# Retention and a bilinear feed-forward in one kernel: 64-token chunks in quarters of the array, smaller tiles, stores on another queue

## The chip, the cores and the metric

The kernel runs on one core of a Trainium2 chip. A core has a matrix engine (TensorE, PE in the profile; its weight loads are shown as PEld), three engines for elementwise work (VectorE or DVE, ScalarE or ACT, GpSimd or POOL), a sync engine (SP) that here only issues DMAs, and 16 DMA engines behind the queues. Every engine works through its own instructions in order; semaphores tie them together. The metric is the device time of one execution in microseconds; shorter is better.

## The reference

The first half is a linear attention with decay (retention): 4 batches, 8 heads, 768 tokens, head size 64. The second half is a feed-forward without a nonlinearity other than a product.

```python
gamma = 1.0 - 2.0 ** (-5.0 - np.arange(H))
for t in range(S):
    state = gamma * state + einsum('bhd,bhe->bhde', k[:, :, t], v[:, :, t])
    y[:, :, t] = scale * einsum('bhd,bhde->bhe', q[:, :, t], state)
x = y.transpose(0, 2, 1, 3).reshape(B * S, H * D)   # 3072 x 512
out = ((x @ w_a) * (x @ w_b)) @ w_out               # d_ff = 1536
```

Inputs and output are float32; the kernel multiplies in bfloat16.

## The kernel before, in words

**Slots.** The 3072 tokens are cut into 24 slots of 128 tokens (six for each batch). The decay is put into the operands: k is multiplied by a table of gamma to the power of minus the position, q by the inverse table and the scale, so that the recurrence becomes a plain sum. For a slot, three products are wanted. `scores` (L252) multiplies transposed k and q of the slot, and DVE applies the causal mask while it copies the result out of PSUM (L257, tile aT). `update` (L268) adds the slot's k-v product to the running state of the batch, and a copy (`cast`, L179 on ACT, L181 on DVE) makes a bfloat16 version of it, gst. `inter` (L288) multiplies q by the state from the slots before, `intra` (L297) the masked scores by v; both add into the PSUM tile y. `leave` (L306) copies y on ACT into xt, the transposed input of the feed-forward. Slots 0 to 5 are handled in pairs by other functions (`scores2`, `update2` and so on), which the change leaves alone.

**Where the operands come from.** SP loads k, q and v of a slot (L91), POOL scales k and q (L209, tile kqb) and copies v (L181): `casts`. The transposed form kqT is made in one of two ways. For slots below `ON_PE` = 10, `flip` transposes on TensorE (L234, L236) and DVE copies the result (L238). For the others `casts` issues a DMA transpose on SP (L223), and behind it the loads of slot t + 2. The first loads, up to slot 11, are issued early and in the order of `LOADS`. There are buffers for the raw loads of three pairs of slots, and for six slots of kqb, v and kqT.

**Feed-forward.** `TILES` = 4, 2, 4, 4, 4, 4, 2 groups the slots into tiles of 512 or 256 tokens. For each tile J and each of twelve blocks ft of the 1536 inner columns, `ffn_ab` makes a (four matmuls L446, copied to asb by ACT, L449) and g (four matmuls L456), and DVE multiplies them into ht (L458). Then `ffn_out` makes 128 tokens of the output for each slot i of the tile (twelve matmuls L481), ACT copies them to osb (L179), and a store follows. All of a, g, o, the flips' results and part of the scores share the PSUM pool psff with three buffers of one bank, in turn.

**Order.** Each engine's order is the order of the calls: `seq` ties every instruction to the one before it on its engine. Attention for slots 6 to 23 runs in blocks, `turn(new, old)`: update and scores for the two slots from `new`, inter and intra for the two from `old`, which had their scores in the block before. A hand-written list says before which call of `ffn_ab` or `ffn_out` each block and each flip stands; `run` puts the casts up to four calls ahead of the flip.

**Stores.** For J < 2 they are held and issued by SP at the next call (`store`, L469); after that they are issued at once on ACT's queue (L491), so they stand among ACT's copies. osb has four buffers.

Of the kernel before, what the change touches and what calls it, by code (L numbers as in the profile page):

```python
# [24 lines left out]
def kernel(  # L25
# [38 lines left out]
    osbp = ctx.enter_context(tc.tile_pool(name="osbp", bufs=4))  # L64
# [98 lines left out]
    mask = const.tile([P, 1, P], BF16, name="mask")  # L163
    gst = [const.tile([P, HP, D], BF16, name=f"gst{i}") for i in range(4)]

    def late_tables():
        seq(nc.gpsimd.memset(mask, 1.0))
        seq(nc.gpsimd.affine_select(out=mask, in_=mask, compare_op=ALU.is_ge, fill=0.0, base=0,
                                    pattern=[[0, 1], [1, P]], channel_multiplier=-1))
        tables([[P, NCH], [0, 1]], 1)  # L170
# [45 lines left out]
    def casts(t):  # L216
# [4 lines left out]
        if t >= ON_PE:  # L221
            kqT[t] = tra.tile([P, 2, HP, P], BF16, tag="kqT", name="kqT", bufs=6)
            seq(nc.sync.dma_start_transpose(  # L223
                out=kqT[t].rearrange("p a b c -> p (a b) c"),
                in_=kqb[t].rearrange("p a hp r d -> p (a hp r d)")))
            if t + 2 < NSLOT:
                load_slot(t + 2)

    def flip(t):
        if t >= ON_PE:  # L230
            return
# [11 lines left out]
    def scores(t, ff):  # L243
        if ff:
            at = [psff.tile([P, HP, P], F32, tag="ff", name=f"at{r}") for r in range(2)]
        else:
            both = psat.tile([P, 2, HP, P], F32, tag="at", name="at")
            at = [both[:, r] for r in range(2)]
        for hp in range(HP):
            for c in range(2):  # L250
                for r in range(2):
                    seq(nc.tensor.matmul(at[r][half(c), hp, :], kqT[t][half(r), 0, hp, half(c)],  # L252
                                         kqT[t][half(r), 1, hp, :], start=True, stop=True,
                                         skip_group_check=True))
        aT[t] = tra.tile([P, 2, HP, P], BF16, tag="aT", name="aT")
        for r in range(2):
            seq(nc.vector.tensor_tensor(aT[t][:, r], at[r], mask.to_broadcast([P, HP, P]), op=ALU.mult))  # L257

    def update(t, eng):
        ci = t % NCH  # L260
        if ci == NCH - 1:
            return
        if ci == 0:
            state[0] = psst.tile([P, HP, D], F32, tag="st", name="st")
        st = state[0]
        for hp in range(HP):
            for r in range(2):
                seq(nc.tensor.matmul(st[half(r), hp, :], kb[t][:, hp, r, :],  # L268
                                     vb[t][:, HP * r + hp, :],
                                     start=(ci == 0 and hp == 0), stop=(hp == HP - 1),  # L270
                                     skip_group_check=True))
        cast(eng, gst[(t + 1) % 4], st)
# [3 lines left out]
    def begin(t, *q):  # L276
        fresh = (t // 2, *q) not in begun
        begun.add((t // 2, *q))
        return fresh

    def inter(t):
        if t % NCH == 0:
            return
        for j in range(2):
            for c in range(2):
                for r in range(2):
                    hp = 2 * j + c
                    seq(nc.tensor.matmul(ys[t // 2][r][half(c), 2 * (t % 2) + j, :],  # L288
                                         gst[t % 4][half(r), hp, :], kqT[t][half(r), 1, hp, :],
                                         start=begin(t, c, r), stop=False, skip_group_check=True))  # L290

    def intra(t):
        for r in range(2):
            for j in range(2):
                for c in range(2):
                    hp = 2 * j + c
                    seq(nc.tensor.matmul(ys[t // 2][r][half(c), 2 * (t % 2) + j, :],  # L297
                                         vb[t][:, HP * r + hp, :], aT[t][:, r, hp, :],
                                         start=begin(t, c, r), stop=True, skip_group_check=True))

    def leave(t):
        J, i = where[t]
        if i == 0:
            xt[J] = xtp.tile([P, KT, 4 * P], BF16, tag="xt", name="xt")
        for r in range(2):
            seq(nc.scalar.copy(  # L306
                xt[J][:, 2 * r : 2 * r + 2, i * P : (i + 2) * P].rearrange(
                    "p j (s n) -> p j s n", s=2),
                ys[t // 2][r].rearrange("p (s j) n -> p j s n", s=2)))

    def turn(new, old, eng=nc.scalar):
        if old is not None:
            ys[old // 2] = [psat.tile([P, 4, P], F32, tag=f"y{r}", name="y") for r in range(2)]
        if new is not None:
            update(new, eng)
            scores(new + 1, True)
            scores(new, False)
        if old is not None:
            inter(old)
            inter(old + 1)  # L320
        if new is not None:
            update(new + 1, nc.scalar)
# [307 lines left out]
```

## Time and profile before

| | |
|---|---|
| median of 3 runs | 233.76 us (233.73 to 234.46) |
| the profiled execution | 235.14 us, of which the span of the instructions is 233.4 us |
| mean granted TensorE clock | 1.000 |
| PE, DVE, ACT, POOL busy | 97%, 41%, 36%, 33% of the span |
| moved by DMA | 38.59 MB in 91894 packets |

The page gives the busy time of each engine and a strip of 40 slices, in which each digit is the busy share in tenths. Groups of instructions have the kernel's line, engine, operation, tiles written and read, shapes, count, busy time, the mean of one, and the idle time of the engine before them with what ended it. A timeline has the start, the busy time, the engine and line, and the count of merged instructions. On lines of a queue (SPq, ACTq) the time is that which issuing the DMA took.

### The profile page before, as it was taken

Reading aid. Unit: us, or ns where it says so; the run is one execution under the profiler, and the core shown is the slowest. Engines: PE = TensorE matmul, PEld = TensorE weight load, DVE = VectorE, ACT = ScalarE, POOL = GpSimd, SP = SyncE. Lnnn points to the kernel's source line nnn. Section 1 sums busy time; section 2 is a strip of 40 time slices with the busy share of each in tenths; the row PEclk is TensorE's granted clock in tenths of the full one; section 3 lists DMA queues with packets and bytes.
Section 4 is the critical chain, followed back from the end, with each engine's and each line's share of the span. In section 5 each row is a group of like instructions: output and inputs, shape, how many; then the busy total and the mean of one; then the engine's idle time right before and its main releaser. Section 6 shows DMA issues by size and latency. Waiting matters only on the chain.

```text
span 233.4 us, 5089 instructions
## 1 busy us (share of the span) xinstructions
PE 226.6 (97%) x2094; PEld 125.8 (54%) x2094; DVE 95.7 (41%) x170; ACT 84.5 (36%) x166; POOL 77.4 (33%) x100
## 2 busy tenths in 40 slices
PE   7999999999999999999799999999999999999995
PEld 6667445686554444545354544454544444445874
DVE  3785267543642274614164630164720233310530
ACT  3454436342134433414244523353422343322422
POOL 4347666788664336444454530000000000000000
PEclk9999999999999999999999999999999999999999
DMA  6999999999999999999999972200002200012102
GB/s 173 290 332 352 341 278 361 363 212 222 204 195 263 277 217 228 177 220 220 249 243 203 234 113 90 93 1 3 0 3 90 90 0 3 0 45 90 48 0 90
DMA packets 91894, 38.59 MB, mean 165 GB/s; under 512 B 71776, under 2 KB 87392, under 8 KB 91872
## 3 DMA queue, kind: packets, MB, share of 16 engines
q1 hardware_dynamic: 89280, 33.69, 64.8%
q10 hardware_dynamic: 2592, 4.59, 5.9%
q8 instruction: 16, 0.26, 0.5%
q14 instruction: 6, 0.05, 0.1%
HBM read 28.31 MB, written 6.29 MB: 148 GB/s over the span
## 4 chain that ended last, share of the span: by engine, by line
PE 74%; DMA 10%; SPq 7%; POOL 3%; ACT 1%; issue 1%; DVE 1%; ACTq 0%; POOLq 0%
PE g L456 22%; PE a L446 21%; PE o L481 19%; DMA kf<-in_k_dram 8%; SPq L223 4%; PE idle L432 4%; SPq L91 3%; POOL kqb L209 3%; DMA qf<-in_q_dram 2%; PE at L252 1%; PE y L297 1%; PE y L412 1%; PE tp L348 1%; PE st L268 1%; PE at L364 1%
## 5 line engine op out<-in xcount | busy, mean ns | idle before, releaser
L458 DVE TENSOR_TENSOR ht<-g,asb 128x512 bf16<-128x512 f32 (+1 forms) x86 | 52.0, 605 | 108.9 <-PE g L456 83.7
L456 PE MATMUL g<-xt,wb_bf 128*128 128x512 bf16 (+1 forms) x344 | 75.4, 344 | 1.6 <-ACT asb L449 1.4
L446 PE MATMUL a<-xt,wa_bf 128*128 128x512 bf16 (+1 forms) x344 | 75.9, 345 | 0.4 <-DVE xt L181 0.3
L449 ACT CAST asb<-a 128x512 bf16<-128x512 f32 (+1 forms) x86 | 44.2, 517 | 72.2 <-PE a L446 69.1
L481 PE MATMUL o<-wo_bf,ht 128*128 128x512 bf16 (+2 forms) x312 | 64.2, 363 | 0.0
L456 PEld LDWEIGHTS <-wb_bf 128*128 128x128 bf16 x344 | 33.6, 98 | 30.2 <-issue 2.1
L446 PEld LDWEIGHTS <-wa_bf 128*128 128x128 bf16 x344 | 32.7, 98 | 28.1 <-DVE xt L181 0.6
L481 PEld LDWEIGHTS <-ht 128*128 128x128 bf16 x312 | 29.2, 98 | 31.5
L209 POOL TENSOR_TENSOR kqb<-kf,ktab 128x512 bf16<-128x512 f32 x22 | 22.9, 1043 | 33.9 <-DMA kf<-in_k_dram 33.4
L179 ACT COPY osb<-o 128x512 f32<-128x512 f32 (+2 forms) x25 | 14.1, 565 | 53.5 <-PE o L481 41.5
L257 DVE TENSOR_TENSOR aT<-at,mask 128x512 bf16<-128x512 f32 x36 | 22.3, 682 | 0.0
L209 POOL TENSOR_TENSOR kqb<-qf,qtab 128x512 bf16<-128x512 f32 x18 | 18.8, 1043 | 3.9 <-DMA qf<-in_q_dram 3.1
L181 POOL CAST vb<-vf 128x512 bf16<-128x512 f32 x24 | 14.5, 612 | 11.6 <-DMA vf<-in_v_dram 9.8
L432 PE MATMUL idle<-zero 128*128 128x256 f32 x30 | 10.4, 487 | 1.6 <-DVE zero L125 1.3
L306 ACT CAST xt<-y 128x512 bf16<-128x512 f32 x18 | 9.7, 589 | 3.0 <-PE y L297 3.0
L432 PEld LDWEIGHTS idle<-zero 128*128 128x128 f32 x30 | 6.7, 243 | 2.9 <-DVE zero L125 1.2
L370 DVE TENSOR_TENSOR aT<-at,mask 128x512 bf16<-128x512 f32 x12 | 7.4, 683 | 1.2 <-PE at L364 1.2
L181 POOL CAST wa_bf<-wsta 128x1024 bf16<-128x1024 f32 (+1 forms) x7 | 6.4, 920 | 3.5 <-DMA wsta<-in_moe_w_a_dram 3.5
L181 POOL CAST wb_bf<-wstb 128x1024 bf16<-128x1024 f32 (+1 forms) x7 | 6.4, 920 | 3.4 <-DMA wstb<-in_moe_w_b_dram 3.4
L181 POOL CAST wo_bf<-wsto 128x1024 bf16<-128x1024 f32 x6 | 6.3, 1042 | 2.4 <-DMA wsto<-in_moe_w_out_dram 2.4
L179 ACT CAST gst<-st 128x256 bf16<-128x256 f32 x12 | 4.5, 372 | 6.7 <-PE st L268 6.7
L252 PE MATMUL at<-kqT 64*64 64x128 bf16 x288 | 5.8, 219 | 0.0
(51 smaller groups left out, 86.8 us busy)
## 6 DMA issues: line engine op xcount, KB each, us to landing
kf<-in_k_dram SPq DMA_DIRECT2D x18, 256.0 KB, 4.3
qf<-in_q_dram SPq DMA_DIRECT2D x18, 256.0 KB, 4.9
vf<-in_v_dram SPq DMA_DIRECT2D x18, 256.0 KB, 5.0
out_dram<-osb ACTq DMA_DIRECT2D x17, 256.0 KB, 2.0
wsta<-in_moe_w_a_dram SPq DMA_DIRECT2D x6, 512.0 KB, 8.7
wstb<-in_moe_w_b_dram SPq DMA_DIRECT2D x6, 512.0 KB, 8.7
wsto<-in_moe_w_out_dram SPq DMA_DIRECT2D x6, 512.0 KB, 9.4
kf<-in_k_dram SPq DMA_DIRECT2D x3, 512.0 KB, 7.1
```

The lines of the kernel that those rows point to most:

```text
L179: seq(nc.scalar.copy(dst, src))
L181: seq(engine.tensor_copy(dst, src))
L209: seq(eng.tensor_tensor(dst, src, tab, op=ALU.mult))
L223: seq(nc.sync.dma_start_transpose(out=kqT[t].rearrange("p a b c -> p (a b) c"), in_=kqb[t].rearrange("p a hp r d -> p (a hp r d)")))
L257: seq(nc.vector.tensor_tensor(aT[t][:, r], at[r], mask.to_broadcast([P, HP, P]), op=ALU.mult))
L306: seq(nc.scalar.copy(xt[J][:, 2 * r : 2 * r + 2, i * P : (i + 2) * P].rearrange("p j (s n) -> p j s n", s=2), ys[t // 2][r].rearrange("p ( ...
L432: seq(nc.tensor.matmul(idle[:, : 2 * P], zero[:, :P], zero, start=True, stop=True, skip_group_check=True))
L446: seq(nc.tensor.matmul(a, wa_bf[:, kt, fs], xcols(J, kt, c0, c1), start=(kt == 0), stop=(kt == KT - 1)))
L449: seq(nc.scalar.copy(asb, a))
L456: seq(nc.tensor.matmul(g, wb_bf[:, kt, fs], xcols(J, kt, c0, c1), start=(kt == 0), stop=(kt == KT - 1)))
L458: seq(nc.vector.tensor_tensor(ht[J][:, ft, c0:c1], g, asbs.pop((J, ft, c0)), op=ALU.mult))
L481: seq(nc.tensor.matmul(o, ht[J][:, ft, i * P : (i + 1) * P], wo_bf[:, ft, c0:c1], start=(ft == 0), stop=(ft == NFT - 1)))
```

## The change

It has five parts.

- From slot 6 on, the attention works on 64-token chunks. `chunk_states` replaces `update`: it makes the k-v product of each of the four chunks in two PSUM tiles (one from the pool psst, one from psff), and DVE adds each product to the running sum, kept in float32 in SBUF. The copy to gst (now eight buffers) is put on a list, `later`. `scores` makes only the 64 x 64 diagonal parts; the mask is 64 columns wide. `inter` and `intra` give each half of the slot its own PSUM bank, y0 or y1. All these matmuls use 64 rows by 64 columns of the array and 64 moving columns.
- `inter` is called twice. In the first call (`swap`) the upper rows of the array write the bank of the second chunk and the other way round; in the second call each writes its own. Between them stands `fenced`: a copy of one column on ACT (on DVE in one block) that waits for the last matmul of the first call, and for which the first matmuls of the second call wait. `chunk_states` and `scores` of the new pair stand in between.
- `later` is worked off by `catch_up`: two entries after each `ffn_ab`, all at `ffn_out` and at the next block. `leave` is put there too.
- Tiles are 4, 2, 2, 2, 2, 4, 4, 4 slots, and a new table `ahead` says what stands before which call: (J, ft) is `ffn_ab`, (J, "o", i) is `ffn_out`. Stores of all but the last two tiles are held and issued by SP at the next call; those of the last two tiles are issued by SP at once, except one part of the very last. osb lives in the buffers of the weight loads, eight in all.
- `ON_PE` is 8: slots 8 and 9 get DMA transposes. The first loads end with slot 10, and behind the transpose of slot t come the loads of slot t + 3.

```diff
-TILES = [4, 2, 4, 4, 4, 4, 2]
+TILES = [4, 2, 2, 2, 2, 4, 4, 4]
-ON_PE = 10
+ON_PE = 8
-LOADS = "p0 p1 w0 w1 w2 w3 w4 p2 w5 o0 o1 o2 o3 o4 o5 s6 s7 s8 s9 s10 s11".split()
+LOADS = "p0 p1 w0 w1 w2 w3 w4 p2 w5 o0 o1 o2 o3 o4 o5 s6 s7 s8 s9 s10".split()
...
-            if t + 2 < NSLOT:
-                load_slot(t + 2)
+            if t + 3 < NSLOT:
+                load_slot(t + 3)
...
+    def catch_up(n=100):
+        for fn in later[:n]:
+            fn()
+        del later[:n]
...
+    def chunk_states(n):
+        u = [psst.tile([P, 2, HP, D], F32, tag="st", name="st"),
+             psff.tile([P, 2, HP, D], F32, tag="ff", name="st")]
+        for s in range(2):
+            for hp in range(HP):
+                for c in range(2):
+                    if (n + s + 1) % NCH == 0 and c == 1:
+                        continue
+                    for r in range(2):
+                        seq(nc.tensor.matmul(u[c][half(r), s, hp, :], kb[n + s][half(c), hp, r, :],
+                                             vb[n + s][half(c), HP * r + hp, :],
+                                             start=True, stop=True, skip_group_check=True))
+        for s in range(2):
+            t = n + s
+            sums[t] = tra.tile([P, 2, HP, D], F32, tag="qk"[s] + "T2", name="sums", bufs=2)
+            for c in range(2):
+                if (t + 1) % NCH == 0 and c == 1:
+                    continue
+                new = sums[t][:, c]
+                old = sums[t][:, 0] if c else sums.get(t - 1, sums[t])[:, 1]
...
+                    seq(nc.vector.tensor_tensor(new, u[c][:, s], old, op=ALU.add))
+                later.append(lambda i=2 * t + c + 1, new=new: cast(nc.scalar, gst[i % 8], new))
...
+    def scores(n):
+        at = psat.tile([P, 2, 2, HP, D], F32, tag="at", name="at")
...
+                        seq(nc.tensor.matmul(at[half(c), r, s, hp, :],
+                                             kqT[n + s][half(r), 0, hp, half(c)],
+                                             kqT[n + s][half(r), 1, hp, half(c)],
+                                             start=True, stop=True, skip_group_check=True))
...
+    def fenced(eng):
+        bi = seq(eng.copy(mark, bq) if eng is nc.scalar else eng.tensor_copy(mark, bq))
+        tc.add_manual_dep(bi.ins, last[mybir.EngineType.PE].name, after, reason="rows change banks")
+        return bi.ins
...
+    def inter(o, swap):
+        for s in range(2):
+            for j in range(2):
+                for r in range(2):
+                    c = 1 - r if swap else r
+                    t = o + s
+                    if t % NCH == 0 and c == 0:
+                        continue
+                    for hp in (2 * j, 2 * j + 1):
+                        into(o, c, r, seq(nc.tensor.matmul(
+                            ys[o][c][half(hp % 2), s, 2 * r + j, :], gst[(2 * t + c) % 8][half(r), hp, :],
+                            kqT[t][half(r), 1, hp, half(c)], start=begin(o, c, hp % 2), stop=False,
+                            skip_group_check=True)))
...
     def turn(new, old, eng=nc.scalar):
+        catch_up()
         if old is not None:
+            ys[old] = [psat.tile([P, 2, KT, D], F32, tag=f"y{c}", name="y") for c in range(2)]
+            inter(old, True)
+            fence[old, 0] = fence[old, 1] = fenced(eng)
         if new is not None:
+            chunk_states(new)
+            scores(new)
+        if old is not None:
+            inter(old, False)
+            intra(old)
             for c in range(2):
+                later.append(lambda c=c: leave(old, c))
...
-        osb = osbp.tile([P, DM], F32, tag="osb", name="osb")
+        osb = wstage.tile([P, DM], F32, tag="w" + "ab"[i % 2], name="osb")
...
-            if J < 2:
+            if J < len(TILES) - 2:
                 held.append((dst, src))
             else:
-                seq((nc.sync if c0 else nc.scalar).dma_start(out=dst, in_=src))
+                seq((nc.scalar if ends and not c0 else nc.sync).dma_start(out=dst, in_=src))
...
+    ahead = {
+        (1, 6): [(casts, 6)], (1, 9): [(flip, 6), (casts, 7)], (0, "o", 0): [(flip, 7)],
+        (0, "o", 1): [(turn, 6, None)], (0, "o", 2): [(casts, 8)], (0, "o", 3): [(casts, 9)],
+        (1, "o", 1): [(turn, 8, 6, D_), (casts, 10)],
+        (2, 2): [(casts, 11)], (2, 7): [(casts, 12)], (2, "o", 0): [(turn, 10, 8), (casts, 13)],
+        (3, 0): [(casts, 14)], (3, 6): [(casts, 15)], (3, "o", 0): [(turn, 12, 10), (casts, 16)],
+        (4, 0): [(casts, 17)], (4, 6): [(turn, 14, 12), (casts, 18)],
+        (4, "o", 0): [(turn, 16, 14), (casts, 19)], (4, "o", 1): [(casts, 20)],
+        (5, 2): [(casts, 21)], (5, 5): [(turn, 18, 16), (casts, 22)], (5, 8): [(casts, 23)],
+        (5, "o", 0): [(turn, 20, 18)], (6, 6): [(turn, 22, 20)], (6, "o", 0): [(turn, None, 22)],
+    }
```

More of the change, by code (lines that the diff above doesn't have):

```diff
@@ L274 @@
-    ys, begun = {}, set()
[L276 to L284, printed above, removed]
-            for c in range(2):
[L286 to L290, printed above, removed]
@@ L311, in turn @@
[L311 to L322, printed above, removed]
[L323 to L326 removed]
+    later = []
```

151 lines of the change are left out of this document (69 added, 82 removed).

## The prediction

> **What bounds the kernel now.** I read the page first (parts 1 and 2), then the groups of instructions by form, then the timeline of TensorE around the attention work, and last the timelines of SP and ACT.
>
> ```profile
> span 233.4 us, 5089 instructions
> PE 226.6 (97%) x2094; PEld 125.8 (54%) x2094; DVE 95.7 (41%) x170; ACT 84.5 (36%) x166; POOL 77.4 (33%) x100
> ...
> PEclk9999999999999999999999999999999999999999
> DMA  6999999999999999999999972200002200012102
> ```
>
> TensorE is busy in 97% of the span at the full granted clock, and no other engine in half of it. The DMA engines are nearly full for the first 23 of 40 slices, about 134 us. So two things can set the time: how long TensorE needs for its work, and whether data reach it in time in the first 134 us.
>
> ```profile
> L481 PE MATMUL o<-wo_bf,ht 128*128 128x512 bf16 x276 | 61.6, 379 | 0.0
> L458 DVE TENSOR_TENSOR ht<-g,asb 128x256 bf16<-128x256 f32 x28 | 11.9, 425 | 22.6 <-PE g L456 11.5 <-ACT asb L449 11.1
> L257 DVE TENSOR_TENSOR aT<-at,mask 128x512 bf16<-128x512 f32 x36 | 22.3, 682 | 0.0
> L179 ACT COPY osb<-o 128x128 f32<-128x128 f32 x1 | 0.3, 266 | 1.0 <-PE o L481 1.0
> ```
>
> A mean duration of a matmul holds its way through the array, so what counts is the distance between starts. The timeline of TensorE in one full attention block (slots 18, 19 with 16, 17) shows it; columns are start, busy us, instruction and count:
>
> ```profile
> 130.07 0.38 PE L456 MATMUL g<-xt,wb_bf 128*128 128x512 bf16 x1
> 130.38 0.32 PE L268 MATMUL st<-vb,kqb 128*64 128x64 bf16 x8
> 130.63 0.64 PE L252 MATMUL at<-kqT 64*64 64x128 bf16 x32
> 131.10 0.39 PE L288 MATMUL y<-kqT,gst 64*64 64x128 bf16 x16
> 131.42 0.32 PE L268 MATMUL st<-vb,kqb 128*64 128x64 bf16 x8
> 131.57 0.62 PE L297 MATMUL y<-aT,vb 128*64 128x128 bf16 x16
> 132.12 0.39 PE L446 MATMUL a<-xt,wa_bf 128*128 128x512 bf16 x1
> ```
>
> The block takes 132.12 - 130.38 = 1.74 us, and the last g matmul before it holds 0.31 where one of 512 columns needs 0.216: 0.09 more on entering the block. The busy time per window of all eleven blocks after slot 5 (the first, the last, and the sum of widths):
>
> ```profile
> 60.88:61.96 1.08, 1.08 (x49) 0.89 (x49) 0.73 (x2) 0.59 (x1) 1.08 (x2) 1.00 1.13 257
> 189.19:190.11 0.92, 0.92 (x34) 0.74 (x33) 0.69 (x1) 0.00 (x1) 0.00 (x0) 1.00 0.00 0
> sum 15.40, PE 15.37 PEld 13.12 DVE 12.05 ACT 6.29 POOL 6.19; mean PE 1.40 PEld 1.19 DVE 1.10 ACT 0.57 POOL 0.56
> ```
>
> With entries that is 15.40 + 11 x 0.09 = 16.4 us of TensorE, and PE fills it.
>
> **The change part by part. A, the quarters.** Every attention matmul becomes 64 rows by 64 columns of the array with 64 moving columns, four at a time. Count for slots 6 to 23: chunk_states 264, scores 288, inter 264 (both calls), intra 288: 1104, or 276 rounds of four. What does a round cost? No row has four quarters with 64 columns. Upper end: L252 has four quarters with 128 columns, 32 in (131.10 - 130.63) = 0.47 us, eight rounds of about 57 ns with 0.02 of entry. Lower end: 64 x 64 with 64 columns, two quarters at a time:
>
> ```profile
> 38.52 0.42 PE L383 MATMUL st<-vb,kqb 64*64 64x64 bf16 x16
> ...
> L383 PE MATMUL st<-vb,kqb 64*64 64x64 bf16 x80 | 2.2, 193 | 0.0
> ```
>
> The sixteen starts spread over 0.42 - 0.19 = 0.23 us, seven steps of 33 ns for two. Quarters of L252 run beside each other without lengthening a round, so I take 33 ns for four, the row with the same shape: 276 x 0.033 = 9.1 us. With ten blocks entered at 0.09 + 0.02 it is 10.2. A gains 16.4 - 10.2 = 6.2 us; at 57 ns it would be 16.8, a loss of 0.4.
>
> [...]
>
> **B, flips.** Slots 8 and 9 lose eight transposes each on PE and a copy on DVE:
>
> ```profile
> 65.01 0.39 PE L234 MATMUL tp<-ident,kqb 128*128 128x128 bf16 x4
> 65.23 0.39 PE L236 MATMUL tp<-ident,kqb 128*128 128x128 bf16 x4
> 65.45 0.38 PE L481 MATMUL o<-wo_bf,ht 128*128 128x512 bf16 x1
> ```
>
> 65.45 - 65.01 = 0.44 us each, a gain of 0.9. DVE's copy is off the path.
>
> **C, stores leave ACT.** Rows of PE and ACT at two tile ends:
>
> ```profile
> 113.36 1.03 PE L446 MATMUL a<-xt,wa_bf 128*128 128x512 bf16 x4
> 115.63 0.81 PE L456 MATMUL g<-xt,wb_bf 128*128 128x512 bf16 x3 [1.24 <-ACT asb L449]
> ...
> 111.83 0.59 ACT L179 COPY osb<-o 128x512 f32<-128x512 f32 x1 [2.00 <-PE o L481]
> 114.61 0.34 ACTq L491 DMA_DIRECT2D out_dram<-osb  x1
> 114.99 1.07 ACT L449 CAST asb<-a 128x512 bf16<-128x512 f32 x2 [2.57 <-DMA qf<-in_q_dram]
> ...
> 214.73 0.60 PE L456 MATMUL g<-xt,wb_bf 128*128 128x256 bf16 x4
> 215.17 0.60 PE L446 MATMUL a<-xt,wa_bf 128*128 128x256 bf16 x4
> 215.97 0.60 PE L456 MATMUL g<-xt,wb_bf 128*128 128x256 bf16 x4 [0.20 <-ACT asb L449]
> ```
>
> The store issued on ACT waited for the completion of a q load, and the asb copy stood behind it. From a (113.36) to g (115.63) are 2.27 us instead of 4 x 0.216 = 0.86: 1.4 lost. At 215.17 it is 0.80 instead of 0.44: 0.4 lost. On SP, one block later, nothing of ACT stands behind a store: 1.8 gained. It could be 0 if the same copies were late for another reason.
>
> **D, tiles.** One 512-column tile becomes two of 256. Four matmuls take 215.17 - 214.73 = 0.44 against half of 0.864, 0.005 more, for 48 groups of four: 0.2 lost.
>
> **E, the bank fence.** Between the two inter calls ACT (DVE once) must see the last matmul of the first call, copy one column, and release PE. The smallest copy shown is 266 ns for 128 columns; one column cannot be longer. With 0.19 for the matmul to end and about 0.05 at each handover that is 0.45 to 0.55 us. Meanwhile PE starts chunk_states and scores, 14 to 16 rounds, 0.46 to 0.53. So eight fences are hidden (at worst 0.1 each), and the ninth, in the last block with nothing between, costs 0.45. If ACT is late with something else, all of inter and intra wait: nothing in the before trace is on ACT at those moments but asb, which ends before g does.
>
> **F, DVE and the three ff buffers.** chunk_states takes one ff buffer and hands it back after four adds (256 columns, 0.425 by the L458 row), then two aT (0.682), then the next ht. For tiles of 512 PE is busy elsewhere for longer; for the block inside a 256 tile, before (4, 6), it is not. Adds start 0.9 after the block's start (entry 0.11, inter and chunk_states eight rounds each, 0.24 until DVE sees them), end at 2.6, aT at 4.0, ht at 4.4. PE is at the second a at 1.15 + 0.87 = 2.0 and waits 0.6, and at the third a 0.87 after that, waiting 0.9. Some 0.2 for the gst and leave copies on ACT: 1.7, and 0.1 each before (5, 5) and (6, 6): 1.9 lost, between 0 (adds shorter than ht) and 2.5.
>
> **G, where slot 9 comes from.** Rows of PE, POOL and SP, and the landing row of the DMA transposes:
>
> ```profile
> 55.16 2.75 PE L481 MATMUL o<-wo_bf,ht 128*128 128x512 bf16 x12
> ...
> 60.81 1.04 POOL L209 TENSOR_TENSOR kqb<-qf,qtab 128x512 bf16<-128x512 f32 x1
> ...
> 61.41 0.94 SPq L91 DMA_DIRECT2D kf<-in_k_dram  x1
> 63.57 1.14 SPq L91 DMA_DIRECT2D vf<-in_v_dram  x1
> 64.81 1.09 SPq L469 DMA_DIRECT2D out_dram<-osb  x1
> 66.00 1.50 SPq L223 DMA_TRANSPOSE kqT<-kqb  x1
> ...
> DMA to landing us min/median/max: 3.1/4.7/7.9
> ```
>
> Up to the loads of slot 10, SP's order is unchanged and SP is free at 61.4 (61.41 is the first load of slot 11). Behind it stand now: store of (0, o, 0), 1.1; transpose of slot 8, 1.55; loads of slot 11, 64.81 - 61.41 = 3.4; store of (0, o, 1), 1.1; only then the transpose of slot 9, at 61.4 + 7.15 = 68.6, landing 4.7 later at 73.3. POOL had slot 9 ready at 61.9, and ACT the two outputs by 59.0 and 62.2, so the queue alone decides. PE arrives thus: 55.16, flip 7 0.44, five out blocks of 2.59, the first new block with 16 rounds 0.65, makes 69.2; entry, 12 inter matmuls, chunk_states and slot 8's scores add 0.6: 69.8. In the order of instructions scores(9) then holds all of PE: 73.3 - 69.8 = 3.5 us lost. Bounds: none if the issues take 0.5 to 0.6 and the landing 3.1; 6.7 at a landing of 7.9. I take the median. The next pair (10, 11) is due at 87; the same count puts its second transpose at about 81 and 85.5 landed, so it is met by 2 us, later ones by more, since each pair is due about 15 us after its predecessor where SP needs about 5 us a slot.
>
> Sum: A -6.2, B -0.9, C -1.8, D +0.2, E +0.45, F +1.9, G +3.5 = -2.85. The profiled execution took 235.14 us (span 233.4), 1.4 above the median 233.76 of the runs; the terms are differences, so 232.3 against the former and 230.9 against the latter. I forecast 231.0.
>
> **Rivals.** First, on the other side: a round of four keeps a cost set by feeding pairs of weight load and matmul, not by columns. It turns slower where a round exceeds 33 + 2850 / 276 = 43 ns; at L252's 57 the time is 231.0 + 6.6 = 237.6. For it: L252 at eight instructions in 57 ns is the densest long stretch shown, and 33 asks for nearly twice that; a block has 256 instructions. Against it: L252's starts sit 4 apart inside a round, so the array takes them faster than that.
>
> Second, slot 9 is in time: G is 0 to 1, the time 227.5 to 228.5. For it: landings of 3.1 occur; against it: DMA is full there and SP's issues stretched from 0.6 to over 1 us.
>
> Third, the wait of G cools TensorE: the longest gap shown is 1.24 us at a clock of 9 tenths or more, so no row tests 3.5. If the next out block ran at half clock, its 2.59 us would double: 231.0 + 2.6 = 233.6, no change. [...]
>
> Fourth, several fences or F's buffers wait longer than worked out, 2 to 3 us together: 233 to 234.
>
> **How the numbers follow.** Forecast 0.42; slot 9 in time 0.14; slow rounds 0.24 (over 43 ns three quarters of it); clock 0.08; fences and buffers 0.12. About 0.3% (0.7 us) is what a measurement can tell from no change. Faster holds the first, the second and some of the rest: 0.60; same 0.09; slower 0.31. The likeliest case's own range is 229.5 to 232.5. From 228.0 to 236.0 leaves out part of the second case and the slowest rounds.
>
> **What would show it.** A: starts of the score matmuls in a block about 0.26 us apart for 32, and a block of some 1.2 us. C: no wait for ACT at 113 and 215. E: no wait for ACT in blocks but the last. F: waits of about 1.5 us for DVE after the block before (4, 6). G: one wait of 2 to 5 us for the transpose DMA near 70 us. The forecast is wrong if rounds take over 40 ns, if a second transpose is late, or if fences wait in every block.

## The result and the profile after

Over four runs each, the changed kernel takes 231.48 us (230.93 to 231.91) and the kernel before 234.11 us (233.73 to 234.63): a ratio of 0.9883, 95% interval 0.9857 to 0.991. The forecast was 231.0 from 228.0 to 236.0, faster. The sum behind it, though, holds two large errors that nearly cancel: the quarters gained some 2 us less than worked out, and the late transpose of slot 9, which was to cost 3.5 us, cost nothing.

The profiled execution took 231.07 us, 0.4 below its median, where that of before had 235.14, 1.0 above the median of its four runs. So the pair of profiles is 4.1 us apart and the medians 2.6. The page of the changed kernel, parts 1 and 2:

```profile
span 229.2 us, 6225 instructions
PE 222.2 (97%) x2606; PEld 132.4 (58%) x2606; DVE 97.9 (43%) x193; ACT 95.0 (41%) x207; POOL 78.0 (34%) x101
...
PEclk9999999999999999999999999999999999999999
DMA  6999999999599998999999938002200002100022
```

TensorE is still the bound, at the full clock, with 512 more matmuls and 4.4 us less busy time. The DMA strip has dips (5, 8) within its first 20 slices that the strip of before does not have.

**The blocks.** The timeline of TensorE around the block before (5, 5), which answers the one shown of before at 130 us (start, busy us, instruction, count). `chunk_states` is L261 here, `scores` L284, `inter` L325, `intra` L336:

```profile
135.23 1.03 PE L492 MATMUL g<-xt,wb_bf 128*128 128x512 bf16 x4
136.19 0.32 PE L325 MATMUL y<-kqT,gst 64*64 64x64 bf16 x16
136.34 0.43 PE L261 MATMUL st<-vb,kqb 64*64 64x64 bf16 x32
136.59 0.49 PE L284 MATMUL at<-kqT 64*64 64x64 bf16 x32
136.91 0.34 PE L325 MATMUL y<-kqT,gst 64*64 64x64 bf16 x16
137.06 0.51 PE L336 MATMUL y<-aT,vb 64*64 64x64 bf16 x32
137.50 1.04 PE L482 MATMUL a<-xt,wa_bf 128*128 128x512 bf16 x4
```

The entry costs 136.19 - 135.23 - 4 x 0.216 = 0.10, as before. The block then takes 1.31 instead of 1.74. `chunk_states` needs 0.25 for eight rounds of four, 31 ns a round; `scores` needs 0.32, 40 ns a round; `intra` 0.44 with the way out of the block. The starts of single matmuls show why: for about 48 matmuls they come in bursts of four, 3 to 4 ns apart, a burst every 32 ns; after that one by one, 8.3 ns apart, with a step of 17 to 34 ns every so often. Four steps of 8.3 are 33 ns too, so it is the longer steps, here called pauses, that cost. Busy time per window over all ten blocks (first, one full, last, sum of widths):

```profile
58.38:59.08 0.70, 0.70 (x66) 0.66 (x65) 0.18 (x1) 0.55 (x1) 0.47 (x2) 1.00 0.15 34
136.19:137.50 1.31, 1.31 (x130) 1.27 (x129) 1.03 (x3) 0.19 (x1) 0.00 (x0) 1.00 0.00 0
183.43:184.55 1.12, 0.82 (x65) 0.67 (x64) 0.69 (x1) 0.19 (x1) 0.00 (x0) 1.00 0.00 0
sum 11.89, PE 11.59 PEld 11.06 DVE 8.33 ACT 3.54 POOL 1.33; mean PE 1.16 PEld 1.11 DVE 0.83 ACT 0.35 POOL 0.13
```

With ten entries of 0.09 the attention costs 12.8 us of TensorE where it cost 16.4: 3.6 gained, the last fence included.

**The last fence.** The same view at the last block:

```profile
183.43 0.32 PE L325 MATMUL y<-kqT,gst 64*64 64x64 bf16 x16
184.05 0.32 PE L325 MATMUL y<-kqT,gst 64*64 64x64 bf16 x16 [0.30 <-ACT lgr L302]
184.19 0.43 PE L336 MATMUL y<-aT,vb 64*64 64x64 bf16 x32
184.55 1.25 PE L519 MATMUL o<-wo_bf,ht 128*128 128x512 bf16 x5
```

From 183.43 to 184.05 pass 0.62 where sixteen matmuls need 0.15, so 0.45 to 0.5 is lost, as worked out. No other block has a wait for the fence (L302; lgr is the tile that its copy writes). Behind this wait the next 48 matmuls go in clean rounds of 32 ns.

**Slot 9.** SP's issues and TensorE's rows around the first block with scores of slots 8 and 9 (on SP's lines the time is what issuing took):

```profile
59.15 0.36 SPq L506 DMA_DIRECT2D out_dram<-osb  x1
59.60 1.35 SPq L224 DMA_TRANSPOSE kqT<-kqb  x1
...
63.35 0.77 SPq L506 DMA_DIRECT2D out_dram<-osb  x1
64.22 1.44 SPq L224 DMA_TRANSPOSE kqT<-kqb  x1
...
69.99 0.45 PE L284 MATMUL at<-kqT 64*64 64x64 bf16 x32
```

The order is the one worked out, but it stands 4.4 us earlier: the transpose of slot 9 is issued at 64.22, not 68.6, and landed at 69.25, 0.85 us before its scores. SP even waits for ACT's first output from 56.2 to 59.15. The loads in front of it ran faster: the last load of slot 10 landed at 59.47, against 65.06 in the profile of before.

**The ff buffers.** TensorE behind the block before (4, 6):

```profile
114.65 0.60 PE L492 MATMUL g<-xt,wb_bf 128*128 128x256 bf16 x4
115.75 0.61 PE L482 MATMUL a<-xt,wa_bf 128*128 128x256 bf16 x4 [0.50 <-DVE sums L275]
116.19 0.60 PE L492 MATMUL g<-xt,wb_bf 128*128 128x256 bf16 x4
117.27 0.60 PE L482 MATMUL a<-xt,wa_bf 128*128 128x256 bf16 x4 [0.47 <-DVE ht L494]
```

Four matmuls of 256 columns take 0.43 to 0.44, so 115.75 - 114.65 loses 0.66 and 117.27 - 116.19 loses 0.64; a third loss of 0.19 follows at 119.3. Together 1.5 of the 1.9 forecast. The two other blocks named there have no such wait. A new one of 0.11 stands ahead of (2, 0).

At no tile's end does TensorE wait for ACT any more.

### The profile page after: what moved, and what is told of

It reads as the page before. It is cut to its first block, busy times and chain, and to the rows that moved or that the text cites. A ratio compares the mean times of both kernels' runs of the same rounds, so it can differ in the third digit from the quotient of the medians.

```text
span 229.2 us, 6225 instructions
## 1 busy us (share of the span) xinstructions
PE 222.2 (97%) x2606; PEld 132.4 (58%) x2606; DVE 97.9 (43%) x193; ACT 95.0 (41%) x207; POOL 78.0 (34%) x101
## 4 chain that ended last, share of the span: by engine, by line
PE 93%; DVE 4%; issue 1%; ACT 0%
PE o L519 27%; PE g L492 27%; PE a L482 27%; PE idle L468 3%; PE y L325 2%; PE y L336 1%; PE at L284 1%; DVE aT L406 1%; PE st L261 1%; DVE qT L182 1%; PE at L400 1%; DVE kqb L210 1%; PE y L448 1%; PE tp L384 1%; DVE aT L290 1%
## 5 line engine op out<-in xcount | busy, mean ns | idle before, releaser
L494 DVE TENSOR_TENSOR ht<-g,asb 128x256 bf16<-128x256 f32 (+1 forms) x98 | 53.7, 549 | 98.6 <-PE g L492 83.1
L482 PE MATMUL a<-xt,wa_bf 128*128 128x256 bf16 (+1 forms) x392 | 78.0, 323 | 1.3 <-DVE sums L275 0.5
L492 PE MATMUL g<-xt,wb_bf 128*128 128x256 bf16 (+1 forms) x392 | 77.5, 323 | 0.1
L485 ACT CAST asb<-a 128x256 bf16<-128x256 f32 (+1 forms) x98 | 46.4, 473 | 72.6 <-PE a L482 71.9
L482 PEld LDWEIGHTS <-wa_bf 128*128 128x128 bf16 x392 | 37.6, 98 | 26.2 <-issue 1.0
L492 PEld LDWEIGHTS <-wb_bf 128*128 128x128 bf16 x392 | 38.3, 98 | 24.1 <-issue 0.4
L182 POOL CAST vb<-vf 128x512 bf16<-128x512 f32 x24 | 15.4, 649 | 35.2 <-PE y L336 11.2
L180 ACT CAST gst<-sums 128x256 bf16<-128x256 f32 x33 | 12.9, 406 | 4.0 <-DVE sums L275 2.0
L275 DVE TENSOR_TENSOR sums<-st,sums 128x256 f32<-128x256 f32 x30 | 12.7, 423 | 1.4
L468 PE MATMUL idle<-zero 128*128 128x256 f32 x30 | 10.6, 493 | 1.3 <-DVE zero L124 1.3
L290 DVE TENSOR_TENSOR aT<-at,mask 128x512 bf16<-128x512 f32 x18 | 11.5, 679 | 0.0
L406 DVE TENSOR_TENSOR aT<-at,mask 128x512 bf16<-128x512 f32 x12 | 7.4, 681 | 1.0 <-PE at L400 1.0
```

The lines of the kernel that those rows point to most:

```text
L180: seq(nc.scalar.copy(dst, src))
L182: seq(engine.tensor_copy(dst, src))
L275: seq(nc.vector.tensor_tensor(new, u[c][:, s], old, op=ALU.add))
L290: seq(nc.vector.tensor_tensor(aT[n][:, r].rearrange("p s h d -> p (s h) d"), at[:, r].rearrange("p s h d -> p (s h) d"), mask.to_broadcast ...
L468: seq(nc.tensor.matmul(idle[:, : 2 * P], zero[:, :P], zero, start=True, stop=True, skip_group_check=True))
L482: seq(nc.tensor.matmul(a, wa_bf[:, kt, fs], xcols(J, kt, c0, c1), start=(kt == 0), stop=(kt == KT - 1)))
```

## The experiments

Two theories stand against each other on the result. Theory one, from the profile above: the quarters lost 2 us of their gain to a pace that only the first 48 or so matmuls of a block keep, slot 9 is in time, and the waits at (4, 6) are the only large new ones. Its rivals: slot 9 only just hits, by chance of this run; the pace is set by operands and not by supply; the gain of the stores is as large in the median as in one profile.

**The change again, unaltered.**

> The changed kernel once more, unaltered, with a profile beside runs of the kernel before on the same chip. In its first profile the loads landed 4 to 5 us earlier near 55 us than in the profile of before, and slot 9's transpose landed at 69.25, 0.9 us ahead of its use. If the speed of the loads differs from execution to execution, this profile shows the transpose's landing move with the landing of slot 10's last load (59.5 there), and wherever it lands after 70.1, a wait of TensorE at the scores of slot 9 of just that difference; the time then grows by the same. If the early landing belongs to the kernel, the landing is again near 69.3 and the time 0.988 of before.

231.6 us (230.94 to 232.19), ratio 0.9883 (0.9844 to 0.9921). The transpose of slot 9 landed at 69.91 and was used near 70.7: in time by about the same margin. The waits behind (4, 6) were 0.47, 0.64 and 0.19. So the profile of after is no exception.

**Slots 8 and 9 transposed on TensorE again.**

```diff
-ON_PE = 8
+ON_PE = 10
...
-            if t + 3 < NSLOT:
-                load_slot(t + 3)
+        if t >= 8 and t + 3 < NSLOT:
+            load_slot(t + 3)
...
-        (1, "o", 1): [(turn, 8, 6, D_), (casts, 10)],
+        (1, "o", 0): [(flip, 8), (flip, 9)], (1, "o", 1): [(turn, 8, 6, D_), (casts, 10)],
```

> Slots 8 and 9 are transposed on TensorE again, both right before the last output block ahead of their attention block; the loads of slots 11 and 12 stay where they are. Theory one (transpose in time): TensorE does 0.9 us more, the time is 0.9 us above the changed kernel. Theory two (the queue makes the transpose late, as predicted): the wait of up to 3.5 us goes, the time is up to 2.6 us below the changed kernel, and the profile of the unaltered kernel shows that wait.

232.41 us (231.52 to 232.69), 0.9906 (0.987 to 0.9942): 0.8 above the unaltered change on the same chip, though the intervals overlap. In the profile the two flips take from 67.33 to 68.22, 0.89 us of TensorE. So this is the price of the flips and no more. Had the transpose cost a wait, undoing it would have been faster.

**The transpose of slot 9 made late.** Its issue is put behind the loads of slot 12.

```diff
+            if t == 9:
+                load_slot(t + 3)
             seq(nc.sync.dma_start_transpose(
...
-            if t + 3 < NSLOT:
+            if t != 9 and t + 3 < NSLOT:
```

> The changed kernel with the transpose of slot 9 behind the three loads of slot 12 on SP instead of ahead of them. In the two profiles so far it landed 0.8 to 0.9 us ahead of its use near 70 us. Theory (the queue of SP and nothing else decides when slot 9 is there): it starts 3.2 us later and TensorE waits 2.0 to 2.8 us at the scores of slot 9, and the time grows by as much; later transposes stay in time. Rival (slack hidden elsewhere): no wait. If a gap of this length halves the granted clock, the output block behind it takes up to 5.2 us instead of 2.6.

Rows of SP and of TensorE (`scores` is L286 here):

```profile
67.62 1.64 SPq L226 DMA_TRANSPOSE kqT<-kqb  x1
...
69.68 0.32 PE L286 MATMUL at<-kqT 64*64 64x64 bf16 x16
71.44 0.32 PE L286 MATMUL at<-kqT 64*64 64x64 bf16 x16 [1.45 <-DMA kqT<-kqb]
```

The issue is 3.4 us later than in the change, the landing (71.40) only 2.2, since the landing took 3.8 instead of 5.0. The scores of slot 9 stand 71.44 - 69.68 = 1.76 behind those of slot 8, of which 0.12 is work: 1.64 lost, all of TensorE held, a little under what was expected. So the mechanism of the forecast exists, with a threshold: the margin of 0.85 comes off first. The clock stayed full (mean 0.999). The one run took 232.27 us, 1.2 above the profile of the change; its first output block began 0.3 earlier, so about 1.5 came on behind that, which fits the 1.64.

**The block before (4, 6) moved between two output blocks.**

```diff
-        (4, 0): [(casts, 17)], (4, 6): [(turn, 14, 12), (casts, 18)],
+        (3, "o", 1): [(turn, 14, 12)],
+        (4, 0): [(casts, 17)], (4, 6): [(casts, 18)],
```

> The attention block of slots 14, 15 with 12, 13 stands ahead of the second output block of tile 3 instead of ahead of (4, 6) in a 256-column tile; nothing else is changed. Theory (the ff buffer held by the four adds makes TensorE wait when only short matmuls follow): the waits of 0.66, 0.64 and 0.19 us after that block go, and the time is 1.4 to 1.5 us below the changed kernel. Rival (DVE is behind there for another reason, or the wait comes back after the output blocks): 0 to 0.5 us below.

230.76 us (229.94 to 232.06), 0.9853 (0.9805 to 0.9901); the medians are 0.84 apart. The three waits are gone, and two smaller ones come up earlier:

```profile
105.02 0.32 PE L261 MATMUL st<-vb,kqb 64*64 64x64 bf16 x16
105.51 0.32 PE L261 MATMUL st<-vb,kqb 64*64 64x64 bf16 x16 [0.17 <-POOL vb L182]
...
111.27 0.60 PE L492 MATMUL g<-xt,wb_bf 128*128 128x256 bf16 x4
111.96 0.60 PE L482 MATMUL a<-xt,wa_bf 128*128 128x256 bf16 x4
```

The block now stands so early that `chunk_states` of slot 15 waits for POOL's copy of v: the second half starts 0.49 behind the first, where half of `chunk_states` needs 0.14 to 0.15, so 0.34 is lost. And 111.96 - 111.27 = 0.69 instead of 0.44, 0.25 lost, where ACT is behind with the output copies and ht comes late. So 1.5 - 0.34 - 0.25 = 0.9 by the rows, which agrees with the 0.84 by the medians.

**The stores back on ACT's queue.**

```diff
-            if J < len(TILES) - 2:
+            if J < 2:
...
-                seq((nc.scalar if ends and not c0 else nc.sync).dma_start(out=dst, in_=src))
+                seq((nc.sync if c0 else nc.scalar).dma_start(out=dst, in_=src))
```

> From tile 2 on stores are issued at once on the queue of ACT again, with the eight output buffers of the changed kernel. Theory (a store on ACT waits for an earlier DMA and holds up the asb copy): waits of TensorE for ACT come back at tile ends, one to three of 0.4 to 1.4 us, and the time is 1 to 2 us above the changed kernel. Rival (four output buffers were the cause, not the queue): no such wait and the same time within 0.4 us.

232.25 us (231.68 to 232.74), 0.9908 (0.9875 to 0.9941), 0.65 above the unaltered change. ACT's and TensorE's rows at one tile end:

```profile
91.38 0.34 ACTq L529 DMA_DIRECT2D out_dram<-osb  x1
91.76 0.65 ACT L485 CAST asb<-a 128x256 bf16<-128x256 f32 x2 [0.41 <-PE g L492]
...
91.40 0.60 PE L482 MATMUL a<-xt,wa_bf 128*128 128x256 bf16 x4
92.18 0.49 PE L492 MATMUL g<-xt,wb_bf 128*128 128x256 bf16 x3 [0.18 <-ACT asb L485]
```

The asb copy stands behind the store, and TensorE loses 92.18 - 91.40 - 0.43 = 0.35; another 0.31 is lost at 109.17. The mechanism is the one forecast, at less than the 1 to 2 us expected: here no store waited for the completion of a load (the one above is issued at 91.38, right behind its copy, 90.77 + 0.58). The trace of before shows one that does: the store at 114.61 and the q load issued at 109.18 count their completion on the same semaphore (104 in that trace), the load lands at 114.54, and ACT waits for its count until 114.56 before it issues the store. In this run the DMA that had a store's semaphore before it was issued 7 us or more ahead of the store each time, and had landed.

**The stores alone, in the kernel before.** Held and issued by SP one block later there, and nothing else changed.

```diff
-            if J < 2:
+            if J < len(TILES) - 1:
...
-                seq((nc.sync if c0 else nc.scalar).dma_start(out=dst, in_=src))
+                seq((nc.scalar if ends and not c0 else nc.sync).dma_start(out=dst, in_=src))
```

> The kernel before with one part of the change: stores of all tiles but the last on SP at the next call, those of the last at once on SP; attention, tiles, transposes and the four output buffers are as before. Theory (part C): the waits of 1.4 us near 114 and 0.4 us near 215.5 go, the time is 1.5 to 1.8 us below before. Rival: stores on SP hold up the loads and transposes behind them, so that gains are given back in waits for a transpose or a load, and the time is within 0.7 us of before.

233.37 us (233.22 to 233.88, ten runs) against 234.41 (233.64 to 235.95, seventeen), 0.9958 (0.9938 to 0.9978). TensorE at the tile end where before had lost 1.4 us:

```profile
113.34 1.03 PE L446 MATMUL a<-xt,wa_bf 128*128 128x512 bf16 x4
114.20 1.03 PE L456 MATMUL g<-xt,wb_bf 128*128 128x512 bf16 x4
```

The step from the second a to its g, 2.27 before, is 0.86, with no wait, and so are the next ones. Output buffers are still four here, and in the run above, with eight, TensorE still waited: the queue is the cause, not the buffers. The gain is 1.04 in the median, not 1.5 to 1.8: what the waits cost in the kernel before differs from run to run (the runs spread over 2.3 us, without them over 0.7), and the profile shown there is one of the dear ones.

**Blocks cut in two.** The blocks before (5, 5), (6, 6) and (6, "o", 0) end after `scores`; the second `inter` and `intra` follow one call of the feed-forward later. (`turn` is cut into two functions for that, `first` and `second`.)

```diff
-        (5, 5): [(turn, 18, 16), (casts, 22)], ...
+        (5, 5): [(first, 18, 16)], (5, 6): [(second, 16), (casts, 22)], ...
-        (5, "o", 0): [(turn, 20, 18)], (6, 6): [(turn, 22, 20)], (6, "o", 0): [(turn, None, 22)],
+        (5, "o", 0): [(turn, 20, 18)], (6, 6): [(first, 22, 20)], (6, 7): [(second, 20)],
+        (6, "o", 0): [(first, None, 22)], (6, "o", 1): [(second, 22)],
```

> The last three attention blocks of the changed kernel are each cut in two between the scores and the second inter call, with one feed-forward call (or output block) between the halves. In the unaltered kernel matmuls come in bursts of four, 32 ns a round, for the first 48 of a block, and one by one, 8.4 ns apart with gaps of some 25 ns, after that. Theory (instructions are supplied no faster than that, and the head start is a queue that fills during long matmuls): the second halves now go in bursts, inter and intra starting within 0.41 us instead of about 0.5; each cut costs 0.12 for one more entry and about 0.07 for one more exit, and the last block no longer waits 0.45 for its fence: in all 0 to 0.3 us less than the changed kernel. Rival (inter and intra are slow in themselves, by their operands): the second halves stay at one by one.

231.54 us (231.14 to 231.78), 0.9875 (0.9843 to 0.9907): no difference. The second half of the first block cut:

```profile
138.84 0.32 PE L325 MATMUL y<-kqT,gst 64*64 64x64 bf16 x16
138.99 0.46 PE L336 MATMUL y<-aT,vb 64*64 64x64 bf16 x32
139.38 0.39 PE L488 MATMUL a<-xt,wa_bf 128*128 128x512 bf16 x1
```

The same `intra` on the same operands takes 139.38 - 138.99 = 0.39 with the way out instead of 0.44, and its first 23 matmuls come in bursts of four again: so the slow pace goes by how many matmuls came before, not by what they read. A cut block loses that gain to a second entry (0.10) and a second way out. The last block no longer waits for its fence, which is worth 0.27 there.

**Both repairs.** The block moved as above, and the last block cut around the first output block.

```diff
-        (4, 0): [(casts, 17)], (4, 6): [(turn, 14, 12), (casts, 18)],
+        (3, "o", 1): [(turn, 14, 12)],
+        (4, 0): [(casts, 17)], (4, 6): [(casts, 18)],
...
-        ... (6, "o", 0): [(turn, None, 22)],
+        ... (6, "o", 0): [(first, None, 22)], (6, "o", 1): [(second, 22)],
```

> The changed kernel with the block of slots 14, 15 ahead of the second output block of tile 3, and the last block cut in two around the first output block of tile 6, so that its fence is hidden. Theory: 0.9 us from the first (as measured) and 0.45 less one more entry and exit, 0.25, from the second: 1.1 us below the changed kernel, ratio to before about 0.984.

230.66 us (230.11 to 231.63), 0.9846 (0.9817 to 0.9876): better than the kernel before. Against the change the ratio is 0.004 lower, but the intervals overlap; the moved block alone had 0.9853, so what cutting the last block adds is not shown by the times.

**Why the loads were faster: the buffers shifted by 128 bytes.** The change loads the same things by the same queue, so why do they land earlier? What differs is where the buffers lie. The narrower mask takes 128 bytes a partition less, so all that is allocated behind it, the load buffers among it, starts 256 bytes past a multiple of 512 where it started 384 past before (these are the addresses of the built programs). An unused tile puts them back.

```diff
+    const.tile([P, 64], BF16, name="pad")
```

> The changed kernel with an unused 128 bytes a partition ahead of the weights, raw loads and operands, so that every load buffer begins 384 bytes past a multiple of 512, as in the kernel before, instead of 256 past it. Nothing else differs. In all profiles so far of kernels with before's addresses the 512 KB loads land 1.8 us apart at the start (5.0, 6.9, 8.7, 10.5), and in those with the changed kernel's 1.5 to 1.6 (4.7, 6.2, 7.7, 9.3), on two chips. Theory (the offset of the buffers sets the speed of the loads, and the early landing of slot 9 comes from it): loads 1.8 us apart again, slot 10's last load lands at about 65 instead of 60, slot 9's transpose at 72 to 74, TensorE waits 2 to 3.5 us at the scores of slot 9, and the time is 1.5 to 3.5 us above the changed kernel. Rival (chance, or another part of the change): loads 1.5 to 1.6 us apart and the same time.

236.8 us (235.4 to 237.59) against 234.42 (233.68 to 236.15): 1.0076 (1.0032 to 1.012), slower than before. An unused tile of 128 bytes undoes the whole gain and more. SP's first issues, of the change and then of the shifted kernel:

```profile
6.50 1.45 SPq L96 DMA_DIRECT2D vf<-in_v_dram  x1
7.99 1.45 SPq L104 DMA_DIRECT2D wsta<-in_moe_w_a_dram  x1
```

```profile
6.81 1.74 SPq L96 DMA_DIRECT2D vf<-in_v_dram  x1
8.59 1.74 SPq L104 DMA_DIRECT2D wsta<-in_moe_w_a_dram  x1
```

The first loads of 512 KB land at 4.9, 6.4, 7.9, 9.5 and 11.0 in the change, 5.2, 7.0, 8.7, 10.6 and 12.4 here, and 5.0, 6.9, 8.7, 10.5 and 12.3 in the kernel before: 1.5 us each against 1.8. What follows is the forecast's term G in full, and its third rival, the clock, behind it. SP, then TensorE (lines are one higher here), then windows of 3 us (after the width: busy us and count of PE, PEld, DVE, ACT, POOL; then granted clock, DMA share, GB/s):

```profile
62.65 1.38 SPq L225 DMA_TRANSPOSE kqT<-kqb  x1
...
69.28 1.51 SPq L225 DMA_TRANSPOSE kqT<-kqb  x1
...
70.01 0.32 PE L285 MATMUL at<-kqT 64*64 64x64 bf16 x16
73.58 0.43 PE L285 MATMUL at<-kqT 64*64 64x64 bf16 x16 [3.25 <-DMA kqT<-kqb]
...
78.35 0.60 PE L483 MATMUL a<-xt,wa_bf 128*128 128x256 bf16 x4
...
72.00:75.00 3.00, 1.42 (x61) 1.08 (x63) 1.09 (x3) 0.89 (x3) 0.70 (x3) 0.76 1.29 256
75.00:78.00 3.00, 2.78 (x10) 1.21 (x10) 0.34 (x1) 0.72 (x2) 2.63 (x3) 0.67 1.20 292
```

The transpose is issued at 69.28 (forecast 68.6) and lands at 73.53 (forecast 73.3); the scores of slot 9 stand 3.57 behind those of slot 8 in the row, and TensorE loses 3.45. Then the granted clock falls, to a mean of 0.76 and 0.67 in the last two windows; at half clock that is (0.24 + 0.33) x 3 / 0.5 = 3.4 us. Half fits the first matmul of the next output block: it takes 0.61 where the mean in the change is 0.379, which is 0.23 more, about its 0.216 once again. That block, 2.71 long in the change, takes 3.78. So (2, 0) begins at 78.35 instead of 73.52, 4.83 later. Another loss of 1.3 follows behind the block before (5, 5), in the middle of four a matmuls:

```profile
141.89 0.51 PE L337 MATMUL y<-aT,vb 64*64 64x64 bf16 x32
142.32 0.10 PEld L483 LDWEIGHTS <-wa_bf 128*128 128x128 bf16 x1
...
143.80 0.82 PE L483 MATMUL a<-xt,wa_bf 128*128 128x512 bf16 x3 [1.41 <-issue]
```

The first of the four weight loads stands at 142.32, the other three matmuls begin at 143.80, and the profile names no releaser for them (issue). A 16 KB packet of instructions was fetched there (on the queue whose packets grow from 16 to 20 with the change as TensorE's loads and matmuls grow from 4188 to 5212). It started at 141.3, inside the block, where in the change the packet with that place in the program starts at 134.8, ahead of the block; that the wait is for it was not tried. Together 4.83 and 1.3 are the 6.1 us by which this profiled run, 237.2 us, is above that of the change. Of the five runs four have a mean clock of 0.991 to 0.993; the fifth has 1.000 and took 235.4.

**The kernel before, shifted.** The same line in the kernel before puts its buffers on multiples of 512.

> The kernel before with an unused 128 bytes a partition at the same place, so that its load buffers begin at multiples of 512 bytes. Theory (the offset sets the speed of the loads): loads land 1.5 to 1.6 us apart at the start and the first loads of slots 6 to 11 land 4 to 5 us earlier; TensorE had all its data in time before, so the time falls by no more than the waits behind stores on ACT do, 0 to 1.8 us. Rival: loads 1.8 us apart as in before, the same time.

234.59 us (233.62 to 235.01) against 234.42, 0.9994 (0.9972 to 1.0016). The loads land at 4.8, 6.3, 7.8, 9.3 and 10.8, as fast as in the change, and the time is the same: TensorE has its data in time there either way. The profiled run, 233.63 us, lacks the wait of 1.4 behind a store on ACT, since the load with that store's semaphore was issued at 102.19 instead of 109.18 and had landed; the median does not show that as a gain. So the placing gives nothing by itself; in the changed kernel it decides whether slot 9 is in time.

**Both repairs, shifted.** The pad is 256 bytes here, and the buffers lie on multiples of 512.

```diff
+    const.tile([P, 128], BF16, name="pad")
```

> The combination of the moved block and the cut last block, with an unused 256 bytes a partition, so that the load buffers begin at multiples of 512 instead of 256 past one. If only the odd 128 bytes matter, loads and time are as without it (0.985 of before); if a multiple of 512 matters too, the loads land closer together than 1.5 us, and the time stays within 0.5 us, since no load is waited for.

230.0 us (229.53 to 232.07), 0.9815 (0.9778 to 0.9851). Its loads land as in the unshifted one (4.8, 6.2, 7.7, 9.2), and the intervals of the two overlap: no further gain is shown.

## Why the prediction was right, and where its sum was wrong

- **A, quarters (-6.2).** This term was mis-sized: -4.1 (-3.6 measured with the last fence in it, which is E's 0.45). The round of 33 ns was right as long as it lasted: bursts of four every 32 ns. It failed as a row for 32 rounds in a stretch: it came from eight rounds of L383, and behind the first 48 or so matmuls a block goes by one load and matmul at a time, with pauses. That looks like the first rival's mechanism (pairs are fed more slowly than the array takes them), at a fraction of its price: 38 to 42 ns a round in the second half of the block before (5, 5), ways out apart, not 57 throughout. Of the 2.1 us, ten ways out of a block are 1.1 (the next matmul starts 0.118 behind the last of the block, where the pace is 0.008); they stand in the 16.4 of before, and the sum for after had entries alone. The pauses are the other 1.0. By the forecast's own sign this term was wrong: without the fence's wait the ten windows hold 11.43 us for 276 rounds, 41 ns each with the ways out, and the sign was 40. In the block before (5, 5) a round, with its four weight loads, takes 31 to 42 ns.
- **B, flips (-0.9).** Right: undoing it cost 0.8 by the medians, 0.89 by the rows.
- **C, stores (-1.8).** Right in place, and as large in that pair of profiles; in the median the stores alone gave 1.04 and in the changed kernel 0.65. The rows were those of one execution in which the waits were long. The term wanted the median of many executions, which one profile does not give.
- **D, tiles (+0.2).** Nothing contradicts it (0.43 to 0.44 for four matmuls of 256).
- **E, last fence (+0.45).** Right: 0.45 to 0.5, and none in the other blocks.
- **F, ff buffers (+1.9).** Right in place and releaser, 1.5 in size. The third wait was 0.19, and (5, 5) and (6, 6) have none. Moving the block away took 0.84 off the median.
- **G, slot 9 (+3.5).** This step failed, by its start and not by its count. "Up to the loads of slot 10, SP's order is unchanged and SP is free at 61.4" took the issue times of before for loads that land in other places. With the buffers put back by 128 bytes the transpose is issued at 69.28 and TensorE loses 3.45, as worked out. As it is, slot 9 lands 0.85 before its use, and the second rival, with a chance of 0.14, was what happened to this term.
- **The third rival, the clock.** It happened where the wait was there: 3.45 us idle, then by the two windows above some 3.4 us of half clock. The price was some 1.4 and not 2.6: no run shows half clock over a whole output block. If it was one stretch at half, it began as the scores went on (0.24 x 3 / 0.5 = 1.4 us of it lie before 75.0, so from 73.6), and ended at 77.0; the output block began at 74.58, so 2.4 us of it fell there and cost that block 1.07; the rest fell on the scores, inter and intra ahead of it. A wait of 1.64, in the run with the late transpose, left the clock full (mean 0.999). What length of wait it takes, between these two, is not shown.

The sum by the measured terms is -3.6 - 0.9 - 1.8 + 0.2 + 1.5 + 0.1 = -4.5, where A and E are the -3.6 and 0.1 is the wait ahead of (2, 0). The first output block starts at 55.70 instead of 55.16, but 0.44 of that is flip 7, which the change puts ahead of this block and the kernel before put behind it; 0.1 is a later start. That makes -4.4, and the spans differ by 4.2. Against the medians C is nearer 1.0, which leaves -3.6 to compare with the measured -2.6. The start of single runs explains a part of the difference: the unaltered change, profiled again at 231.72 us, began its first output block at 56.32, 0.6 later. The other 0.4 is not traced.

So the number was hit by luck: A's missing 2.1 and F's and C's small errors met G's missing 3.5. Had G been set to 0 from the start, with the other terms as they were, the forecast would have been 227.5, 4 us below the measured time.

## What to carry to other kernels

Take the issue time of a load only for as long as its destination stays where it was: a constant that becomes smaller (here by 128 bytes a partition) moves every buffer behind it, and a transfer with a margin of under 1 us (here 0.85) then hangs on that. Price a long run of small matmuls by a row of the same length, and count the way into and the way out of it each time (here 0.10 and 0.11 us). A wait that stands in one profile only, before a store or behind a DMA, is to be weighed by the spread of the runs before it is put into a sum.

## What the runs showed of the hardware

**The place of a load's destination in SBUF set its speed here.** With buffers at 256 or 0 bytes past a multiple of 512, the loads of 512 KB of k, q or v land 1.5 us apart in the first 12 us; at 384 past, 1.8. The pages of the change and of the shifted kernel show it over the whole span, for the same packets and bytes (queue, packets, MB, share of 16 engines' span):

```profile
q1 hardware_dynamic: 93840, 38.68, 67.0%
```

```profile
q1 hardware_dynamic: 93840, 38.68, 75.0%
```

0.670 x 229.2 = 154 us against 0.750 x 235.4 = 177 us, 15% more. The kernel before and its shifted form repeat it, with the same packets and bytes as each other: 64.8% of 233.4 us is 151 us at 384, 58.2% of 231.9 is 135 at 0. Three kernels with buffers at 384 (before, the stores alone, the shifted change) load slowly, and all with 0 or 256 fast; no other place was tried. The first loads of k, q and v, in packets of 512 bytes by the traces, go from 1.5 to 1.8 us apart, those of the first weights, in packets of 1 KB, from about 1.35 to 1.5 (the change against before). Why the place has this effect is not shown.

**The pace of small matmuls had two parts here.** In the block before (5, 5) of the change the first 40 to 48 pairs of load and matmul go in bursts of four every 32 ns, then pairs 8.3 ns apart with pauses of 17 to 34: 31 ns a round of four in the first part, 38 to 42 in the second. A wait of half a microsecond (the last fence) gives back the fast part for 48 more. A stock of instructions made ready ahead is the author's reading of this; the blocks cut in two speak for it (bursts again for 16 and 23 matmuls behind the cut), and no run shows what holds it.

**A program's timing can hang on 128 bytes.** With the load buffers shifted, a change that gains 1.2% loses 0.8%. In the profiled run 4.8 of the 6.1 us come from one transpose that lands 4.3 us later and the clock that falls behind it.
